# LSH attention, softplus-gated feed-forward and eight experts on one core: fewer weight blocks decoded during attention, feed-forward begun in two groups of two

## The chip, the cores and the metric

One core of a Trainium2 chip runs the whole program in one launch. The metric is device time in microseconds (us) of the launch; the kernel before takes 1490.02 us (median of 3 runs, 1488.71 to 1490.52). The engines are named as the profile names them: PE (matrix multiply, with PEld for its weight loads), DVE (vector), ACT (scalar, activations), POOL (GpSimd), SP (issues DMAs).

## The reference, cut to what matters

Three stages follow each other: hash-bucketed attention over 16 heads (2 x 8, 768 positions, 64 dimensions), a dense feed-forward whose two weight matrices arrive as float64, and eight experts weighted by a Sinkhorn-normalised gate.

```
mask   = q_bucket[..., :, None] == k_bucket[..., None, :]      # 6 sign bits
attn   = softmax(where(mask, q k^T / 8, -1e9))                 # + 1e-09 in the denominator
x      = (attn v) as [1536, 512]
h      = x @ w_in                                              # w_in  float64 [512, 2048]
x      = (h * tanh(softplus(h))) @ w_out                       # w_out float64 [2048, 512]
P      = sinkhorn(x @ w_gate, 8 rounds)
out    = sum over 8 experts of P[:, e] * (relu(x @ w1[e]) @ w2[e])
```

The change touches the attention and the feed-forward. The experts, which follow, are not touched.

## The kernel before, in words

**Attention.** Work is cut into 32 units (a head and one half of its 384 queries) and 16 pairs of units. Per unit, `s_mm` (L378, tile `ps`) and `s_max` (L383, `mx`) find the row maxima, `rows_mm`/`rows_cp` bring them into one row, `st_mm` (L413 and L414, `pst`) makes six blocks of transposed scores, `st_exp` (L419, ACT) writes their exponentials into a ring of NP tiles `p`, POOL adds three blocks at a time into `pa` (L431, `add`), and `av_mm` (L441, `pav`, twelve matmuls for a pair and half the keys) and `sum_mm` (L451, `psum`) multiply by v and by ones. `norm` then divides: part 0 transposes the sums, part 1 copies neighbouring 32-partition groups on ACT into `other` (L463), part 3 adds EPS, `other` and the own half and inverts (L465, L466), parts 4 to 7 spread, multiply and split the result into a rounded high part and the rest (`xh`, `xl`).

**What sets the order there.** The attention is a list of tasks with engine, cost, due time and predecessors; a planner inside the kernel simulates the engines and emits the tasks in the order of its simulated start plus DELTA times the due time. OFF holds an offset of the due time for each kind of task. So a change in OFF, DELTA, DUE0 or PACE moves instructions on every engine, and each engine then runs its queue in that order.

**Float64 blocks.** The feed-forward's weights are 16 blocks (128 hidden columns of `w_in`, the same rows of `w_out`). A block comes in two halves of 512 KB into `stage` (three buffers, next load issued when a half is decoded). `decode(i, j, part)` takes integers apart: parts 0 and 1 on ACT (L146, L148), parts 2 to 5 on DVE (L150, L152, L154, L158), part 6 on POOL (L160), part 7 a sum into `dec` (L162, DVE or POOL in attention, DVE later). When both halves are there, `convert_hi` (ACT, L174) rounds the block into the ring of weights, and `convert_lo` (POOL, L180) writes the rest beside it. The attention decodes NATT = 4 blocks, that is 8 halves, as tasks of its planner.

**Feed-forward.** Tokens are three tiles of 512 (`tb`), blocks are taken in groups of FG = 4. A step n is one block on one token tile: `up(n)` is 12 matmuls (L784 and L785 with the high part of the block, L786 with its low part) into `h`; `act(n)` runs Mish and the rounding on ACT (L794, L795, `gh`) and the difference on DVE (L796, `gl`); `down(n)` is 12 matmuls into four accumulators `y` (L809). `down` runs LAG = 3 steps behind `up`. After the last block of a group, `evacuate` moves the four `y` to `final`: by ACT copies for group 0 (L817), by DVE additions for later groups (L819). Here the order is that of the loops over n, word for word: decode parts of a half are put at the step `int(nd)`, where nd grows by 1.35 per half, and the conversion of a block at the end of a later step. In the loop:

```
        if n < NST:
            up(n)
            for t in early.pop(n, []):
                decode(*t)
        first = n >= LAG and step(n - LAG)[4]
        if first:
            down(n - LAG)
        if n < NST:
            act(n)
```

`first` is the case in which step n - 3 ends a group: its `down` and the evacuation then stand ahead of `act(n)`. Ahead of the loop, block 3 is converted.

Of the kernel before, what the change touches and what calls it, by code (L numbers as in the profile page):

```python
# [7 lines left out]
F32 = mybir.dt.float32  # L8
# [8 lines left out]
P = 128  # L17
# [19 lines left out]
NDEC = 4  # L37
NS = 4
NRAW = 2
NP = 13  # L40
NT3 = 3
NPA = 6
AVG = 3
AVD = 9
ENTER = 0.14
LEAVE = 0.2
TURN = 0.1
ADDS = "P"
ADDD = 2
WARM = 5  # L50
FILL = 256
AHEAD = (1, 2)
OFF = {'weight_lo': 36.6, 'add': -4.0, 'weight_load': -13.2, 'norm6': 47.2, 'prep_hi': 0.0, 'norm_move': -42.7, 'load_qk': 1.7, 'norm0': -50.6, 'load_v': -17.1, 'decode': 12.7, 'bits_mm': 4.7, 'norm1': -37.8, 'norm5': 6.7, 'st_exp': -4.0, 'norm7': 30.9, 'rows_cp': -121.7, 'av_mm': -0.2, 'rows_move': -14.2, 'rows_mm': 3.4, 'norm4': -154.4, 'norm3': 4.9, 'sum_mm': -2.0, 'bits_cmp': -19.3, 'av_one': -57.3, 'weight_hi': 177.8, 's_max': 3.7, 'st_mm': 2.6, 'prep_move': 0.2, 'prep_lo': 0.5, 'bits_move': -3.6, 's_mm': 3.0}
DELTA = 0.0397
RECEIPT = 1.6
DIRECT = 4
DUE0 = 20
PACE = 26
NX = 1
NATT = 4  # L60
# [13 lines left out]
def lsh_attention_moe_kernel(  # L74
# [111 lines left out]
    def attention():  # L186
        with ExitStack() as a:
# [23 lines left out]
            xu = out_p.tile([P, 2, HALF], F32, name="xu")  # L211
            rs = out_p.tile([P, S], F32, name="rs")
            nr = out_p.tile([P, HALF // 32], F32, name="nr")
            other = out_p.tile([P, HALF // 32], F32, name="other")
            pj = out_p.tile([P, 12], F32, name="pj")
            pf = sets.tile([P, 4, 32], F32, name="pf")

            ps = [p_p.tile([P, 512], F32, name=f"p{i}") for i in range(NP)]
            pas = [p_p.tile([P, HALF], F32, name=f"pa{i}") for i in range(NPA)]
            warm = []  # L220
            raw_t, hi_t, lo_t, psb_t, bit_t = {}, {}, {}, {}, {}
# [231 lines left out]
            def norm(n, part, e=None):  # L453
                hp, half = divmod(n, 2)
                b, hp = divmod(hp, H // 2)
                c, x = slice(half * HALF, (half + 1) * HALF), xu[:, half, :HALF]
                g = slice(b * S + half * HALF, b * S + (half + 1) * HALF)
                first = rs[:, c].rearrange("p (b j) -> p b j", j=32)[:, :, 0]
                if part == 0:
                    nc.vector.transpose(out=rs[:, c], in_=sum_t[n][:, :HALF])  # L460
                elif part == 1:
                    for y in range(4):
                        nc.scalar.copy(other[32 * y:32 * y + 32], first[32 * (y ^ 1):32 * (y ^ 1) + 32])  # L463
                elif part == 3:
                    nc.vector.scalar_tensor_tensor(out=nr, in0=other, scalar=EPS, in1=first, op0=ALU.add, op1=ALU.add)  # L465
                    nc.vector.reciprocal(out=nr, in_=nr)  # L466
                elif part == 4:
                    nc.vector.transpose(
                        out=rs[:, c].rearrange("p (b j) -> p b j", j=32),
                        in_=nr.unsqueeze(2).to_broadcast([P, HALF // 32, 32]),  # L470
                    )
# [96 lines left out]
            for u in range(NU):  # L568
# [14 lines left out]
                for c in range(NKC):  # L583
                    i = 6 * u + c
                    j = place(u, c) - NP
                    old = order[j + (NKC if j >= NKC else 0)] if u != 1 and j >= 0 else None
                    task("E", i - 4.0, st_mm, u, c, after=ready + ([nm(st_exp, *order[i - NT3])] if i >= NT3 else []) + [nm(bits_cmp, 0, 1, 0)] * (i == 2))
                    read = [av_done(old[0], old[1] // AVG), nm(add, old[0], old[1] // 3, max(old[1] % 3 - 1, 0))] if old else []
# [6 lines left out]
            for n in range(NU // 2):  # L595
                last = n == NU // 2 - 1
                us = members(n)
                due = 6 * us[1]
                room = [nm(norm, n - 1, 5)] if n else []
                for g in range(NKC // AVG):  # L600
                    task("E", due + AVG * g + AVD, av_mm, n, g,
                         after=[nm(st_exp, u, c) for u in us for c in range(AVG * g, AVG * g + AVG)] + ([nm(av_mm, n, g - 1)] if g else room)
                         + [nm(load_v, head(u)) for u in us] + [nm(clear_slots, j) for j in range(3)] * (n < 2))
                task("E", due + 8, sum_mm, n, after=[nm(add, u, g, 1) for u in us for g in range(2)] + [nm(norm, n - 2, 5)] * (n > 1), ring="r", frees=nm(norm, n, 0))
                raw = [nm(bits_mm, x) for x in (1, 2)] + [nm(prep_lo, x, i) for x in (1, 2) for i in range(2)]
                due += 10
                task("D", due, norm, n, 0, cost=0.58, after=[nm(sum_mm, n)] + ([nm(norm, n - 2, 5)] if n > 1 else raw))
                task("A", due, norm, n, 1, cost=0.85, after=[nm(norm, n, 0)] + [nm(norm, n - 1, 3)] * (n > 0))
# [17 lines left out]
            for n in range(NCH):  # L626
# [5 lines left out]
                for part, (e, cost) in enumerate(costs):  # L632
# [4 lines left out]
                        7: [nm(decode, i, j, 6)] + ([nm(weight_lo, i - NDEC, 1)] if i >= NDEC else []) + ([av_done(1, x) for x in range(NKC // AVG)] + [nm(add, 1, g, x) for g in range(2) for x in range(2)] if i < 3 else []),  # L637
                    }[part]
                    task(e, due + 0.3 * part, decode, i, j, part, after=after, cost=cost)
                if j == 1 and i < RING_A + NX:  # L640
                    last = uses(NH - NS + i - RING_A)[1]
                    task("A", due + 5, weight_hi, i, after=[nm(decode, i, x, 7) for x in range(2)] + ([nm(weight_lo, i - 1, 1)] if i else [])
                         + (st_done(last) if i >= RING_A else []))
# [48 lines left out]

            for k, t in tasks.items():
                for d in t[5]:
                    assert d in tasks, (k, d)
                    users.setdefault(d, []).append(k)
                if not left[k]:
                    ready_at[k] = 0.0
                    offer(k)
            count = 0  # L700
            while count < len(tasks):
# [13 lines left out]
                if e == "E":  # L715
                    mode[0] = KIND.get(f, 0)
                if e == "E" and nm(warm_up) in ends:
                    keep_warm(int(max(0.0, real - free[e] - 0.25) / 0.12))
# [14 lines left out]
                for d in users.get(k, ()):  # L733
                    left[d] -= 1
                    if not left[d]:
                        ready_at[d] = max(ends[x] for x in tasks[d][5])
                        offer(d)
                f(*args, *([e] if f in PICK else []))
                count += 1
# [24 lines left out]
    hps, hid, yps = {}, {}, {}  # L764
    NST = NTB * N64

    GROUPS = [list(range(i, i + FG)) for i in range(0, N64, FG)]
    NG = N64 // FG
    turns = [(g, tb) for g in range(NG - 2) for tb in range(NTB)]
    turns += [(g, tb) for g in (NG - 2, NG - 1) for tb in range(2)] + [(g, 2) for g in (NG - 2, NG - 1)]  # L770
    steps = [(g, tb, i) for g, tb in turns for i in GROUPS[g]]
# [253 lines left out]
    nxt = 0  # L1025
    nd = 0.0
    free_dec = {}
    convert_hi()
    convert_lo()
    for i in range(RING_A + NX + 1, N64):  # L1030
        need = free[i - RING] + 1 if i >= RING else 0
        if NATT <= i:
            nd = max(nd, free_dec.get(i - NDEC, 0))
            for j in range(2):
                d = int(nd)
                for part, lag in enumerate((0, 0, 0, 0, 0.5, 0.5, 0.5, 1.4)):
# [285 lines left out]
```

## Time and profile before

| what | value |
|---|---|
| median of 3 runs | 1490.02 us (1488.71 to 1490.52) |
| profiled execution | 1490.93 us, its span 1489.1 us |
| PE busy, share of the span | 1476.4 us, 99% |
| DVE, ACT, POOL busy | 871.2, 638.3, 913.9 us |
| attention (first instruction to the first `up`) | 0 to 222.97 us |
| granted PE clock, mean | 0.999 |

PE works nearly all the time, so the end moves by what PE waits, by the clock at which it runs, and by the number of its matmuls. The rows below show where it waits, and what DVE, POOL and ACT do ahead of the places that it may wait for. A matmul's duration covers its way through the array; what it takes of PE's time is the distance between starts.

### The profile page before, as it was taken

To read this page: it belongs to the slowest core of one execution; us is meant where nothing else is said; L and a number is where in the kernel's file an instruction comes from. 1 tells how busy PE (TensorE), PEld (TensorE's weight loads), DVE (VectorE), ACT (ScalarE), POOL (GpSimd) and SP (SyncE) were. 2 spreads that over 40 slices of the span, in tenths; PEclk is the share of its full clock that TensorE was granted. 3 is DMA by queue.
4 is the path that set the end of the run, shared out by engine and by line. 5 is a ranking of instruction groups with operands and counts; after the bars stand their busy time and mean duration, and the time that the engine had idled before them with its cause. 6 is when DMAs were issued, how large, how long until landed. Compare 5 with 4: busy or idle time off the path is not lost.

```text
span 1489.1 us, 20182 instructions
## 1 busy us (share of the span) xinstructions
PE 1476.4 (99%) x7457; PEld 1258.9 (85%) x7457; DVE 871.2 (59%) x1393; ACT 638.3 (43%) x1161; POOL 913.9 (61%) x762
## 2 busy tenths in 40 slices
PE   9999999999999999999999999999999999999998
PEld 6666658888888899998999989999899898998987
DVE  7898888777526666656444476643544435344353
ACT  6566656554324434344343333443334333343331
POOL 7878784333224766666666666666666666666660
PEclk9999999999999999999999999999999999999999
DMA  7755523222100122222122221232112221222211
GB/s 193 195 157 158 135 58 99 72 71 71 57 1 29 57 73 70 71 72 70 59 71 71 72 67 62 71 114 71 65 63 72 71 72 61 67 72 71 72 43 43
DMA packets 66490, 116.70 MB, mean 78 GB/s; under 512 B 18276, under 2 KB 20440, under 8 KB 66392
## 3 DMA queue, kind: packets, MB, share of 16 engines
q1 hardware_dynamic: 66392, 115.43, 25.4%
q8 instruction: 58, 0.95, 0.3%
q14 instruction: 40, 0.33, 0.1%
HBM read 93.41 MB, written 3.15 MB: 65 GB/s over the span
## 4 chain that ended last, share of the span: by engine, by line
PE 96%; DVE 2%; issue 1%; ACT 1%; DMA 1%; POOL 0%; DVEq 0%; ACTq 0%; SPq 0%; POOLq 0%
PE y L1174 35%; PE u L1107 32%; PE y L809 9%; PE pav L441 4%; PE h L786 3%; PE h L784 3%; PE h L785 3%; PE pst L413 2%; PE ps L378 2%; PE pst L414 2%; PE psum L451 1%; DVE mx L383 1%; PE pbits L352 0%; PE lg L837 0%; PE prow L394 0%
## 5 line engine op out<-in xcount | busy, mean ns | idle before, releaser
L1115 ACT ACTIVATE gh<-c 128x384 fp32r<-128x384 f32 x256 | 134.6, 526 | 174.3 <-DVE c L1127 172.2
L1127 DVE TENSOR_TENSOR u<-u,p 128x384 f32<-128x384 f32 x64 | 35.7, 558 | 283.7 <-PE u L1107 283.7
L1120 DVE SCALAR_TENSOR_TENSOR gl<-c,gh 128x384 fp32r<-128x384 f32 x256 | 196.0, 828 | 0.0
L1174 PE MATMUL y<-ww,gh 128*128 128x512 f32 x768 | 186.6, 391 | 0.0
L1174 PE MATMUL y<-w,gh 128*128 128x512 f32 x768 | 186.0, 391 | 0.0
L1174 PEld LDWEIGHTS y<-w,gh 128*128 128x128 f32 x768 | 143.7, 188 | 28.9
L1174 PEld LDWEIGHTS y<-ww,gh 128*128 128x128 f32 x768 | 143.7, 188 | 28.8
L989 POOL TENSOR_TENSOR w<-stage,w 128x1024 fp32r<-128x1024 f32 x32 | 76.3, 2385 | 89.1 <-ACT w L985 89.1
L989 POOL TENSOR_TENSOR ww<-stage,ww 128x1024 fp32r<-128x1024 f32 x32 | 76.3, 2384 | 81.7 <-ACT ww L985 81.7
L809 PE MATMUL y<-gh,w 128*128 128x512 f32 x336 | 109.8, 389 | 0.0
L160 POOL TENSOR_TENSOR stage<-stage,sgn 128x512 f32<-128x512 f32 x32 | 43.5, 1358 | 98.1 <-DVE sgn L158 74.4
L419 ACT ACTIVATE p<-pst 128x384 f32<-128x384 f32 x186 | 82.6, 490 | 46.8 <-PE pst L414 33.3
L985 ACT CAST ww<-stage 128x1024 fp32r<-128x1024 f32 x32 | 33.6, 1052 | 157.5 <-PE y L1174 157.5
L965 POOL TENSOR_TENSOR wa<-stage,wa 128x512 fp32r<-128x512 f32 x32 | 45.6, 1424 | 89.0 <-ACT wa L960 80.0
L985 ACT CAST w<-stage 128x1024 fp32r<-128x1024 f32 x32 | 33.6, 1050 | 154.5 <-PE y L1174 154.5
L1174 PE MATMUL y<-ww,gl 128*128 128x512 f32 x384 | 98.2, 389 | 0.0
L1174 PE MATMUL y<-w,gl 128*128 128x512 f32 x384 | 97.7, 389 | 0.2 <-DVE gl L1120 0.2
L965 POOL TENSOR_TENSOR wx<-stage,wx 128x512 fp32r<-128x512 f32 x32 | 45.4, 1419 | 80.6 <-ACT wx L960 80.6
L383 DVE TENSOR_REDUCE mx<-ps 128x1 f32<-128x768 f32 x96 | 88.3, 948 | 7.9 <-PE ps L378 6.8
L1107 PE MATMUL u<-tw,w 128*128 128x384 f32 x480 | 91.7, 336 | 0.0
L1107 PE MATMUL u<-tw,ws 128*128 128x384 f32 x480 | 91.7, 336 | 0.0
L1174 PEld LDWEIGHTS y<-w,gl 128*128 128x128 f32 x384 | 72.0, 188 | 15.5 <-DVE gl L1120 0.6
(206 smaller groups left out, 3651.1 us busy)
## 6 DMA issues: line engine op xcount, KB each, us to landing
stage<-in_w_dram SPq DMA_DIRECT2D x160, 512.0 KB
raw<-in_qk_dram SPq DMA_DIRECT2D x13, 384.0 KB
sb<-hi SPq DMA_DIRECT2D x20, 192.0 KB
vt<-in_v_dram SPq DMA_DIRECT2D x16, 192.0 KB
out_dram<-acc SPq DMA_DIRECT2D x11, 256.0 KB
wx<-hi SPq DMA_DIRECT2D x14, 192.0 KB
zq<-hi SPq DMA_DIRECT2D x10, 192.0 KB
ak<-hi SPq DMA_DIRECT2D x10, 192.0 KB
```

The costliest lines, as they stand in the source:

```text
L383: nc.vector.tensor_reduce(out=mx_t[u % 2][:, t:t + 1], in_=s_t.pop((u, t))[:, :, :HALF], axis=AX.XY, op=ALU.max, negate=True)
L419: nc.scalar.activation(p_t[u, c][:, :HALF], st_t.pop((u, c))[:, :HALF], AF.Exp, scale=0.125)
L441: nc.tensor.matmul(av_t[n][64 * e:64 * e + 64, :WIDE], vt[head(u) // 2 % 2][:, c, e, :], p_t[u, c][:, :WIDE], start=(c == 0), stop=(c == N ...
L784: nc.tensor.matmul(t, wt[:, 0, f], xh[:, kc, c], start=(kc == 0), stop=False)
L809: nc.tensor.matmul(yps[j], x, y, start=(head and m == 0), stop=(tail and m == 2))
L965: nc.gpsimd.tensor_sub(a[:, 1, 0:512], t[:, 0, :], f32(a)[:, 0, 0:512])
L985: nc.scalar.copy(wbuf[u % 2]["w"][:, 0, :], staged["u", u, 1].rearrange("p c n -> p (c n)"))
L989: nc.gpsimd.tensor_sub(y[:, 1, :], t, f32(y)[:, 0, :])
L1107: nc.tensor.matmul(bank[x], weight(u, a, m, kc), moving(u, b, mm, kc), start=(first and n == 0), stop=(n == 5), skip_group_check=not first)
L1115: nc.scalar.activation(hi, src, AF.Relu)
L1120: nc.vector.scalar_tensor_tensor(out=lo, in0=src, scalar=0.0, in1=f32(hid_u[u, c][0]), op0=ALU.max, op1=ALU.subtract)
L1174: nc.tensor.matmul(y_t[t], (hi, hi, lo)[m][:, t % 3 * P:(t % 3 + 1) * P], y, start=(k == 0 and first), stop=(k == NF // 2 - 1 and last),)
```

## The change

- The attention decodes and converts two blocks in place of four (NATT, and the task of block 2's conversion goes). Blocks 2 and 3 are decoded in the feed-forward loop; nd starts at block 2 and grows by 1.15 per half in place of 1.35. The conversion of block 3 ahead of the loop goes.
- The feed-forward's first group of four blocks becomes two groups of two: block 2 is first used in step 6, block 3 in step 7, block 4 in step 12 (as before) and block 7 in step 15 (as before). There are five groups and so three times four more evacuations; those of the second group are DVE additions, at steps 10, 12 and 14.
- `norm`: the ACT copies write beside the own half in `rs` and add EPS, and part 3 is one reduction over two neighbours; `other` is gone, and with it one wait of part 1.
- The ring of exponentials has 15 places, the two new ones in the fourth `dec` tile. The planner releases a place after the chunk of `av_mm` that reads it, and lets `av_mm` start up to a little ahead of its last exponentials. OFF, DELTA, DUE0 and PACE have new numbers; fewer filler matmuls are laid into PE's gaps in the first 7.5 us of the plan.

```diff
-NP = 13
+NP = 15
-OFF = {'weight_lo': 36.6, 'add': -4.0, 'weight_load': -13.2, ...
-DELTA = 0.0397
+OFF = {'weight_lo': 11.0, 'add': -10.2, 'weight_load': -52.8, ...
+DELTA = 0.0374
-DUE0 = 20
-PACE = 26
+DUE0 = 52
+PACE = 38
-NATT = 4
+NATT = 2
...
-            ps = [p_p.tile([P, 512], F32, name=f"p{i}") for i in range(NP)]
+            ps = [p_p.tile([P, 512], F32, name=f"p{i}") for i in range(NP - 2)] + [dec[3][:, k:k + 512] for k in (0, 512)]
...
-                        nc.scalar.copy(other[32 * y:32 * y + 32], first[32 * (y ^ 1):32 * (y ^ 1) + 32])
+                        z = 32 * (y ^ 1)
+                        nc.scalar.activation(both[32 * y:32 * y + 32, :, 1], both[z:z + 32, :, 0], AF.Copy, bias=EPS)
                 elif part == 3:
-                    nc.vector.scalar_tensor_tensor(out=nr, in0=other, scalar=EPS, in1=first, op0=ALU.add, op1=ALU.add)
+                    nc.vector.tensor_reduce(out=nr, in_=both, axis=AX.X, op=ALU.add)
...
+                    for c in range(AVG * g, AVG * g + AVG):
+                        for u in us:
+                            sooner[nm(av_mm, n, g), nm(st_exp, u, c)] = max(0.0, 0.66 * (c - AVG * g) - SLIP)
...
-                if j == 1 and i < RING_A + NX:
+                if j == 1 and i < RING_A:
...
-    GROUPS = [list(range(i, i + FG)) for i in range(0, N64, FG)]
-    NG = N64 // FG
+    GROUPS = [[0, 1], [2, 3]] + [list(range(i, i + FG)) for i in range(FG, N64, FG)]
+    NG = len(GROUPS)
...
-    convert_hi()
-    convert_lo()
-    for i in range(RING_A + NX + 1, N64):
+    for i in range(RING_A, N64):
...
-                nd += 1.35
+                nd += 1.15
```

Line numbers of the changed kernel are a little higher: L162 is its part 6 on POOL (before: L160), L182 its `convert_lo` (L180), L152, L154, L156, L160 its DVE parts 2 to 5, L164 its part 7, L810 its `gl`, L833 its evacuation by DVE.

**POOL at the start of the feed-forward, before.** `w_2662` and `w_2663` are the ring's places for blocks 4 and 5; the row ahead of these is the conversion of block 3.

```order
L160 TENSOR_TENSOR stage<-stage,sgn_86 128x512
L160 TENSOR_TENSOR stage<-stage,sgn_87 128x512
L160 TENSOR_TENSOR stage<-stage,sgn_86 128x512
L180 TENSOR_TENSOR w_2662<-dec_82,w_2662 128x1024
L160 TENSOR_TENSOR stage<-stage,sgn_87 128x512
L160 TENSOR_TENSOR stage<-stage,sgn_86 128x512
L160 TENSOR_TENSOR stage<-stage,sgn_87 128x512
L180 TENSOR_TENSOR w_2663<-dec_83,w_2663 128x1024
```

The same place in the changed kernel, behind the last `add` of the attention; `wx_78` takes block 2, `w_2614` block 3, `w_2615` block 4.

```order
L162 TENSOR_TENSOR stage<-stage,sgn_86 128x512
L162 TENSOR_TENSOR stage<-stage,sgn_87 128x512
L162 TENSOR_TENSOR stage<-stage,sgn_86 128x512
L162 TENSOR_TENSOR stage<-stage,sgn_87 128x512
L182 TENSOR_TENSOR wx_78<-dec_84,wx_78 128x1024
L162 TENSOR_TENSOR stage<-stage,sgn_86 128x512
L162 TENSOR_TENSOR stage<-stage,sgn_87 128x512
L182 TENSOR_TENSOR w_2614<-dec_85,w_2614 128x1024
L162 TENSOR_TENSOR stage<-stage,sgn_86 128x512
L182 TENSOR_TENSOR w_2615<-dec_82,w_2615 128x1024
```

Before, POOL reached block 4 first; now four halves (all of blocks 2 and 3) stand ahead of the conversion of block 2, and both halves of block 4 ahead of that of block 3.

**DVE in step 14 of the feed-forward, before** (from the `gl` of step 13 to that of step 14 and behind it); `dec_82` and `dec_83` are tiles of blocks 8 and 9, and no evacuation stands here.

```order
L796 TENSOR_TENSOR gl<-t,gh 128x512
L162 TENSOR_TENSOR dec_82<-stage 128x512
L154 SCALAR_TENSOR_TENSOR stage<-stage,sgn_86 128x512
L158 TENSOR_SCALAR sgn_86<-stage 128x512
L150 TENSOR_SCALAR stage<-stage 128x512
L152 TENSOR_SCALAR sgn_87<-stage 128x512
L796 TENSOR_TENSOR gl<-t,gh 128x512
L162 TENSOR_TENSOR dec_83<-stage 128x512
```

The same step in the changed kernel; `dec_85` belongs to block 7, `dec_82` to block 8, `sgn_87` in the last rows to the second half of block 8.

```order
L810 TENSOR_TENSOR gl<-t,gh 128x512
L164 TENSOR_TENSOR dec_85<-stage 128x512
L156 SCALAR_TENSOR_TENSOR stage<-stage,sgn_86 128x512
L160 TENSOR_SCALAR sgn_86<-stage 128x512
L152 TENSOR_SCALAR stage<-stage 128x512
L154 TENSOR_SCALAR sgn_87<-stage 128x512
L833 TENSOR_TENSOR acc<-y_3180,acc 128x512
L833 TENSOR_TENSOR acc<-y_3184,acc 128x512
L833 TENSOR_TENSOR acc<-y_3188,acc 128x512
L833 TENSOR_TENSOR acc<-y_3192,acc 128x512
L810 TENSOR_TENSOR gl<-t,gh 128x512
L164 TENSOR_TENSOR dec_82<-stage 128x512
```

Block 7's last sum has moved into this step's queue, two steps ahead of its first use, and four evacuations (the second group, third token tile) now stand among the decode parts. Behind the last row come parts 4 and 5 of block 8's second half.

**POOL around the conversions of blocks 6 and 7, before**; `w_2664` is block 6, `w_2665` block 7, and the L160 between them are the second half of block 7 and the first of block 8.

```order
L160 TENSOR_TENSOR stage<-stage,sgn_86 128x512
L180 TENSOR_TENSOR w_2664<-dec_84,w_2664 128x1024
L160 TENSOR_TENSOR stage<-stage,sgn_87 128x512
L160 TENSOR_TENSOR stage<-stage,sgn_86 128x512
L180 TENSOR_TENSOR w_2665<-dec_85,w_2665 128x1024
```

The same two conversions in the changed kernel; `w_2617` is block 6, `w_2618` block 7, and the L162 ahead of each are the two halves of blocks 7 and 8.

```order
L162 TENSOR_TENSOR stage<-stage,sgn_86 128x512
L162 TENSOR_TENSOR stage<-stage,sgn_87 128x512
L182 TENSOR_TENSOR w_2617<-dec_84,w_2617 128x1024
L162 TENSOR_TENSOR stage<-stage,sgn_86 128x512
L162 TENSOR_TENSOR stage<-stage,sgn_87 128x512
L182 TENSOR_TENSOR w_2618<-dec_85,w_2618 128x1024
```

Each conversion now stands behind a further half of the block that follows: that of block 7 behind the second half of block 8, whose DVE parts are put into step 14.

## Rows read from the trace of the kernel before

**Rows 1.** Windows: busy us and count of PE, PEld, DVE, ACT, POOL; PE clock; DMA.
```profile
0.00:222.97 222.97, 214.69 (x1290) 138.73 (x1290) 190.40 (x295) 135.74 (x311) 181.98 (x198) 0.99 0.58 150
222.97:260.00 37.03, 36.63 (x161) 29.97 (x161) 33.03 (x46) 24.25 (x42) 17.39 (x12) 1.00 0.30 95
62.00:66.00 4.00, 4.00 (x15) 3.69 (x14) 3.93 (x7) 2.58 (x5) 2.49 (x3) 0.57 0.70 248
```
**Rows 2.** Waits of PE in the attention: us in total, times, longest.
```profile
PE warm L292 <- DVE xh L286: 1.6, 1, 1.6
PE ps L378 <- DMA sb<-hi: 1.3, 1, 1.3
```
**Rows 3.** Timeline of PE in the attention: start us, duration us, instruction.
```profile
155.06 0.34 PE L413 MATMUL pst<-zq,ak 128*128 128x384 f32 x1
...
155.41 0.34 PE L413 MATMUL pst<-zq,ak 128*128 128x384 f32 x1
```
**Rows 4.** Groups of instructions in 0 to 223 us: count, busy us, mean ns.
```profile
L160 POOL TENSOR_TENSOR stage<-stage,sgn 128x512 f32<-128x512 f32 x7 | 9.9, 1413 | 1.6 <-DVE sgn L158 1.6
...
L154 DVE SCALAR_TENSOR_TENSOR stage<-stage,sgn 128x512 int32<-128x512 int32 x8 | 7.9, 984 | 0.1
...
L150 DVE TENSOR_SCALAR stage<-stage 128x512 f32<-128x512 f32 x8 | 6.4, 794 | 0.0
L152 DVE TENSOR_SCALAR sgn<-stage 128x512 int32<-128x512 int32 x8 | 6.3, 785 | 0.1
...
L158 DVE TENSOR_SCALAR sgn<-stage 128x512 int32<-128x512 int32 x8 | 6.1, 757 | 0.1
```
**Rows 5.** Chain of work in the feed-forward: start us, us, what.
```profile
234.82 2.72 PE y L809 x12
240.27 2.72 PE y L809 x12
```
**Rows 6.** Timeline of POOL in the feed-forward.
```profile
235.32 1.38 POOL L160 TENSOR_TENSOR stage<-stage,sgn 128x512 f32<-128x512 f32 x1 [3.15 <-ACT t L794]
239.48 1.31 POOL L160 TENSOR_TENSOR stage<-stage,sgn 128x512 f32<-128x512 f32 x1 [2.78 <-DVE sgn L158]
...
245.08 2.42 POOL L180 TENSOR_TENSOR w<-dec,w 128x1024 fp32r<-128x1024 f32 x1
...
260.42 2.40 POOL L180 TENSOR_TENSOR w<-dec,w 128x1024 fp32r<-128x1024 f32 x1
...
281.53 2.42 POOL L180 TENSOR_TENSOR w<-dec,w 128x1024 fp32r<-128x1024 f32 x1
```
**Rows 7.** Timeline of DVE in the feed-forward.
```profile
233.42 0.69 DVE L796 TENSOR_TENSOR gl<-t,gh 128x512 fp32r<-128x512 f32 x1 [0.51 <-ACT gh L795]
...
239.62 1.46 DVE L152 TENSOR_SCALAR sgn<-stage 128x512 int32<-128x512 int32 x1
...
317.14 2.73 DVE L819 TENSOR_TENSOR acc<-y,acc 128x512 f32<-128x512 f32 x4 [0.24 <-PE y L809]
319.79 0.68 DVE L796 TENSOR_TENSOR gl<-t,gh 128x512 fp32r<-128x512 f32 x1
320.39 0.69 DVE L162 TENSOR_TENSOR dec<-stage 128x512 f32<-128x512 f32 x1
320.99 0.69 DVE L154 SCALAR_TENSOR_TENSOR stage<-stage,sgn 128x512 int32<-128x512 int32 x1
321.71 0.43 DVE L158 TENSOR_SCALAR sgn<-stage 128x512 int32<-128x512 int32 x1
```
**Rows 8.** Timeline of ACT at the start of the feed-forward.
```profile
223.79 0.91 ACT L463 COPY other<-rs 32x12 f32<-32x12 f32 x4 [4.52 <-DVE rs L460]
...
230.84 1.28 ACT L794 ACT_TABLE_LOAD   x1
232.14 0.60 ACT L794 ACTIVATE t<-h 128x512 f32<-128x512 f32 x1
```

More of the change, by code (lines that the diff above doesn't have):

```diff
@@ L44 @@
 AVD = 9
+SLIP = 0.3
 ENTER = 0.14
@@ L50 @@
 WARM = 5
+COLD = 7.5
 FILL = 256
 AHEAD = (1, 2)
-OFF = {'weight_lo': 36.6, 'add': -4.0, 'weight_load': -13.2, 'norm6': 47.2, 'prep_hi': 0.0, 'norm_move': -42.7, 'load_qk': 1.7, 'norm0': -50.6, 'load_v': -17.1, 'decode': 12.7, 'bits_mm': 4.7, 'norm1': -37.8, 'norm5': 6.7, 'st_exp': -4.0, 'norm7': 30.9, 'rows_cp': -121.7, 'av_mm': -0.2, 'rows_move': -14.2, 'rows_mm': 3.4, 'norm4': -154.4, 'norm3': 4.9, 'sum_mm': -2.0, 'bits_cmp': -19.3, 'av_one': -57.3, 'weight_hi': 177.8, 's_max': 3.7, 'st_mm': 2.6, 'prep_move': 0.2, 'prep_lo': 0.5, 'bits_move': -3.6, 's_mm': 3.0}
-DELTA = 0.0397
+OFF = {'weight_lo': 11.0, 'add': -10.2, 'weight_load': -52.8, 'norm6': 87.2, 'prep_hi': 3.9, 'norm_move': -73.0, 'load_qk': -0.2, 'norm0': -29.7, 'load_v': -23.9, 'decode': -0.3, 'bits_mm': 4.8, 'norm1': -110.3, 'norm5': -85.1, 'st_exp': -3.3, 'norm7': 55.1, 'rows_cp': -157.2, 'av_mm': -0.1, 'rows_move': -39.6, 'rows_mm': 3.5, 'norm4': -106.6, 'norm3': 12.6, 'sum_mm': -2.3, 'bits_cmp': -16.6, 'av_one': 12.2, 'weight_hi': 293.4, 's_max': 6.6, 'st_mm': 2.5, 'prep_move': -6.4, 'prep_lo': -4.7, 'bits_move': -9.7, 's_mm': 2.4}
+DELTA = 0.0374
 RECEIPT = 1.6
 DIRECT = 4
-DUE0 = 20
-PACE = 26
+DUE0 = 52
+PACE = 38
 NX = 1
-NATT = 4
+NATT = 2
 FG = 4
@@ L213, in attention @@
             nr = out_p.tile([P, HALF // 32], F32, name="nr")
-            other = out_p.tile([P, HALF // 32], F32, name="other")
             pj = out_p.tile([P, 12], F32, name="pj")
             pf = sets.tile([P, 4, 32], F32, name="pf")
-            ps = [p_p.tile([P, 512], F32, name=f"p{i}") for i in range(NP)]
+            ps = [p_p.tile([P, 512], F32, name=f"p{i}") for i in range(NP - 2)] + [dec[3][:, k:k + 512] for k in (0, 512)]
             pas = [p_p.tile([P, HALF], F32, name=f"pa{i}") for i in range(NPA)]
@@ L457, in norm @@
                 g = slice(b * S + half * HALF, b * S + (half + 1) * HALF)
-                first = rs[:, c].rearrange("p (b j) -> p b j", j=32)[:, :, 0]
+                both = rs[:, c].rearrange("p (b j) -> p b j", j=32)[:, :, 0:2]
                 if part == 0:
@@ L514, in av_done, with av_chunk @@
                 return nm(av_mm, pair_of(u), g)
+            def av_chunk(n, c):
+                return "av_chunk", n, c
+            sooner = {}
             FAST = [("sq", 0)]
@@ L587, in attention @@
                     task("E", i - 4.0, st_mm, u, c, after=ready + ([nm(st_exp, *order[i - NT3])] if i >= NT3 else []) + [nm(bits_cmp, 0, 1, 0)] * (i == 2))
-                    read = [av_done(old[0], old[1] // AVG), nm(add, old[0], old[1] // 3, max(old[1] % 3 - 1, 0))] if old else []
+                    read = [av_chunk(pair_of(old[0]), old[1]), nm(add, old[0], old[1] // 3, max(old[1] % 3 - 1, 0))] if old else []
                     task("A", i - 9.0, st_exp, u, c, after=[nm(st_mm, u, c)] + read)
@@ L607, in attention @@
                 task("D", due, norm, n, 0, cost=0.58, after=[nm(sum_mm, n)] + ([nm(norm, n - 2, 5)] if n > 1 else raw))
-                task("A", due, norm, n, 1, cost=0.85, after=[nm(norm, n, 0)] + [nm(norm, n - 1, 3)] * (n > 0))
+                task("A", due, norm, n, 1, cost=0.85, after=[nm(norm, n, 0)])
                 task("D", due, norm, n, 3, cost=0.45, after=[nm(norm, n, 1)] + [nm(norm, n - 1, 4)] * (n > 0))
@@ L639, in attention @@
                     task(e, due + 0.3 * part, decode, i, j, part, after=after, cost=cost)
-                if j == 1 and i < RING_A + NX:
-                    last = uses(NH - NS + i - RING_A)[1]
-                    task("A", due + 5, weight_hi, i, after=[nm(decode, i, x, 7) for x in range(2)] + ([nm(weight_lo, i - 1, 1)] if i else [])
-                         + (st_done(last) if i >= RING_A else []))
+                if j == 1 and i < RING_A:
+                    task("A", due + 5, weight_hi, i, after=[nm(decode, i, x, 7) for x in range(2)] + ([nm(weight_lo, i - 1, 1)] if i else []))
                     for j in range(2):
@@ L694, in attention @@
                 for d in t[5]:
-                    assert d in tasks, (k, d)
+                    assert d in tasks or d[0] == "av_chunk", (k, d)
                     users.setdefault(d, []).append(k)
@@ L717, in attention @@
                 if e == "E" and nm(warm_up) in ends:
-                    keep_warm(int(max(0.0, real - free[e] - 0.25) / 0.12))
+                    keep_warm(int(max(0.0, real - free[e] - 0.25) / (0.21 if real < COLD else 0.12)))
                 if e == "Q":
@@ L732, in attention @@
                     ring_use[ring].append(frees)
-                for d in users.get(k, ()):
+                made = [k]
+                if f is av_mm:
+                    for x in range(AVG):
+                        made.append(av_chunk(args[0], AVG * args[1] + x))
+                        ends[made[-1]] = real + cost * (x + 1) / AVG + SEEN[e]
+                for d in (d for x in made for d in users.get(x, ())):
                     left[d] -= 1
                     if not left[d]:
-                        ready_at[d] = max(ends[x] for x in tasks[d][5])
+                        ready_at[d] = max(ends[x] - sooner.get((d, x), 0.0) for x in tasks[d][5])
                         offer(d)
@@ L778, in up @@
         g, tb, i, _, _ = step(n)
+        assert i < converted[0]
         wt = ring[i % RING]
```

## The prediction, made before the changed kernel ran

> **What bounds the kernel now.** I read the windows first. In the attention, 0 to 222.97 us, PE is busy for 214.69 us: it stands idle for 8.3 us in all [rows 1]. The waits of PE name them: the longest is 1.6 us for the first memset, which no edit touches; the next is 1.3 us for a DMA of `sb` [rows 2]. Between them PE is really fed: two neighbouring first matmuls of `pst` start 0.35 us apart, with the second one of the pair between them, shot after shot [rows 3]. So the attention holds at most 8.3 - 1.6 = 6.7 us of idle time to win. There is one stretch more: behind the DMA wait the granted clock falls, 0.57 on the mean of 62 to 66 us, so between the levels of 1.2 and 2.4 GHz, worth 4 x 0.43 = 1.7 us [rows 1].
>
> From 222.97 us on PE waits 0.4 us up to 260 [rows 1], and the chain shows `down` after `down` at a distance of 5.44 us: a step is 2.72 us of `up` and 2.72 us of `down`, 0.227 us per matmul [rows 5]. PE sets the end there, and every wait that is put into it is paid in full. I count time t from the first `up` (222.97).
>
> Third, the engines ahead of PE. DVE's parts 2 and 3 wait while POOL multiplies: L152 takes 1.46 us [rows 7] with the L160 of 1.31 us beside it [rows 6], where its sister L158 takes 0.43 [rows 7]. At the start of the feed-forward the two therefore work as one queue. One half of a block takes 4.16 us (L160 at 235.32, then 239.48); between the conversions of blocks 4 and 5, 245.08 and 260.42, three halves, one conversion and their `gl` take 15.34 us [rows 6].
>
> **Attention: what goes.** Four halves leave. DVE loses 4 x (0.984 + 0.794 + 0.785 + 0.757) = 13.3 us, POOL three of seven multiplications, 3 x 1.41 = 4.2 us: 17.5 us of the common queue [rows 4], and ACT loses parts 0 and 1. But PE hardly waited for that queue, so the gain is bounded by PE's own gaps: 6.7 + 1.7, and some 1.5 us of filler matmuls at the start (my estimate), about 10 us at best. The plan is reordered, which can open new gaps: 1 us of loss is the other end. I take 5 us, half of the bound, since the waits on `mx`, `row` and the exponentials are those of the order and not of the decode alone. The `norm` edit (a reduction over 128 x 24 for an addition over 128 x 12, on DVE), the two more places of `p` and the earlier release lie inside the same bound, off PE; I cost them at nothing, and what a longer reduction could cost, some 0.1 us in the last pair, is within the rounding.
>
> **Feed-forward: what comes.** First uses on PE: `up(0..2)` stand alone, then each step is 5.44, so step n begins at 8.16 + 5.44 (n - 3). Block 2 is needed at `up(6)`, t = 24.5, block 3 at 29.9, block 6 at 68.0, block 7 at 73.4, each plus 0.45 since the low part is first used by the third matmul. Before, block 7's low part was written from 281.53 to 283.95 [rows 6], t = 61: 12 us early. Now 17.5 us and the conversion of two blocks more lie ahead of it.
>
> *Block 2.* Before, DVE's first `gl` came at 233.42 [rows 7], and POOL began block 4's conversion 11.66 us later, behind three halves. Now ACT is done with `norm` at 224.70, does a half's parts (1.3), loads the table (1.28) and runs Mish and the rounding (2 x 0.6) [rows 8]: the first `gl` is at about t = 5.5. Four halves stand ahead of the conversion: 5.5 + 11.66 + 4.16 = 21.3, done at 23.7. It is needed at 24.95. No stall, by 1.2 us.
>
> *Block 3.* Two halves lie between, so 15.34 - 4.16 = 11.2 us later: 32.5, done at 34.9; put into DVE's queue instruction by instruction it comes a us earlier. Needed at 30.4: PE waits 3.5 to 4.5, I take 4.
>
> *Block 6.* Its conversion stands behind both halves of block 7, and those behind the evacuation at step 12, after `down(9)`. Counted from the end of `down(5)`: the ACT evacuation ends 0.8 us later (as DVE's does) and `act(8)` takes 1.2, so DVE resumes at +2.0. Up to the end of the conversion DVE and POOL then do 5 `gl` (3.0), 4 sums (2.4), parts 4 and 5 of 5 halves (5 x 1.12), parts 2 and 3 of 4 halves with POOL in the way (4 x 1.86), 2 evacuations (5.4), one last multiplication (1.4) and 2 conversions (4.8): 30.0 [rows 6, 7]. That is +32.0; PE comes there at 10 x 2.72 + 0.45 = 27.65. It waits 4.3 us. Were DVE on time, only the chain behind `down(9)` counts, as for block 7, and leaves 1.0.
>
> *Block 7.* Here the order alone decides. In step 14 DVE must do, behind `down(11)`: four evacuations, `gl`, a sum, parts 4 and 5 of block 8's second half; then POOL multiplies it and only then converts block 7. The same row of work before: evacuation from 317.14, L158 ends at 322.14 [rows 7], while that `down` ends at 234.82 + 15 x 5.44 + 2.72 = 319.1 [rows 5]; so +3.0, then 1.31 and 2.42 [rows 6] and 0.2 for hand-overs: 6.95 us behind `down(11)`. But `up(15)` follows it at once and wants the block after 0.45. PE waits 6.5 us, whatever the speed of DVE before; if DVE is late as for block 6, about a us more.
>
> Sum: 4 + 4.3 + 6.5 = 14.8 us. What such waits do to the clock: behind the wait of 1.3 us above, PE lost 1.7 us at the lower level [rows 1, 2]. I count that once for each of the three waits, 5.2 us; its bounds are 0 and 10. The 0.4 us of rows 1 goes. Feed-forward +19.6, attention -5: +14.6. The twelve additional evacuations cost PE nothing of themselves: the next `down` of a group's head comes 2.72 us later, and the first `y` is free 0.7 us after its evacuation begins.
>
> The skill speaks on the clock: the Trainium skill, "TensorE: Matmul & The Clock Gate", section "Why this matters for your kernels", advises against idle gaps between bursts of matmuls, since a long one puts the clock back to half. Rows 1 and 2 agree for a shorter gap than it names; by the rule all three waits pay, as in my sum, and without it the time would be about 1500.
>
> **Rivals.** *The common queue is the bound of the attention, not PE.* PEld is busy 138.73 of 222.97 us, while DVE is at 190.40 and POOL at 181.98 [rows 1]. If PE's busy time hides waits, all 17.5 us come back in the attention, and the feed-forward, with DVE on time, pays only what the order makes, 6.5 + 1.0: 1490.9 - 17.5 + 7.5 - 0.4 = 1480.5. It decides from where PE's matmuls start further apart than 0.35 us per pair. Against it: the rows of starts. The Trainium skill, "Trainium Kernel Development and Optimization", section "Performance Expectations", bears on this rival: matmul busy time is called a bad measure and the share of LDWEIGHTS a good one; by that, 0.62, PE has room and this rival's time would hold.
>
> *Decode keeps up.* If DVE and POOL interleave better than in rows 6, block 3 is in time and block 6 waits 1.0, the clock holds, and the attention gives 8: 1490.9 - 8 + 7.5 - 0.4 = 1490. For it: the reordering starts DVE 5 us earlier in the feed-forward. Against it: between 235 and 260 us DVE had no room.
>
> *The queue stays full.* From step 16 a block takes 2 x 3.5 + 2.4 of decode, 2.3 `gl` and 2.3/4 of an evacuation, 12.4 us, in 2.3 steps or 12.5 us (3.5 is 4.16 without its `gl`). If any of that is larger, later `gl` and evacuations come late too. Some 8 us more: 1512.5.
>
> **How the numbers follow.** 1490.93 + 14.6 = 1505.5 for the profiled execution, which lay 0.9 above the median of the runs: 1505. Chances: this 0.70 (1495 to 1514 by itself); the common queue 0.15; decode keeps up 0.08; the queue stays full 0.07. The range for 8 in 10 runs from 1489 (attention -10, feed-forward at 8) to 1515. A difference of 0.2%, 3 us, is what a measurement of this kernel tells from no change. Faster 0.16, the first rival and the edge of the second; the same 0.08; slower 0.76.
>
> **What would show it.** Right: the first `up` at 214 to 221 us; PE waiting in the third matmul of `up(7)`, `up(14)` and `up(15)` for POOL's conversion, the last of them 6 us or longer and there even if the other two are not; a granted clock under 1 behind them; no other wait up to the end. Wrong: a first `up` under 210 us (PE did wait for the queue), or blocks 6 and 7 converted ahead of the end of their `down`.

## The result, and the profile after

The changed kernel takes 1505.93 us (median of 4 runs, 1504.85 to 1507.45) against 1489.61 us (4 runs, 1488.71 to 1490.52): a ratio of 1.011, 95% interval 1.0093 to 1.0128. It is slower by 16.3 us; 1505 was forecast. The profiled execution took 1504.85 us, its span 1503.1 us, against 1490.93 and 1489.1 before: 14.0 us more of span, which the rows below account for.

First the waits of PE over the whole kernel (us in total, times, longest):

```profile
PE h L800 <- POOL w L182: 13.5, 3, 6.7
PE ps L379 <- DMA sb<-hi: 2.4, 1, 2.4
PE warm L293 <- DVE xh L287: 1.6, 1, 1.6
```

One row of three waits is new, and it holds 13.5 us: the third matmul of an `up` waits for POOL's `convert_lo`. The other two rows stood before as well [rows 2], the DMA's with 1.3 us. Nothing waits for the twelve additional evacuations.

The windows (busy us and count of PE, PEld, DVE, ACT, POOL; PE clock; DMA share; GB/s) of the attention, and of stretches behind the three waits:

```profile
0.00:219.66 219.66, 212.48 (x1285) 137.85 (x1285) 170.21 (x278) 129.77 (x302) 175.49 (x196) 0.99 0.57 147
256.00:258.00 2.00, 2.00 (x10) 1.66 (x9) 0.31 (x1) 1.57 (x3) 1.31 (x1) 1.00 0.67 250
296.00:298.00 2.00, 2.00 (x8) 1.56 (x7) 1.97 (x5) 0.00 (x0) 0.05 (x1) 0.64 0.19 23
298.00:300.00 2.00, 2.00 (x6) 1.55 (x5) 1.50 (x2) 0.59 (x1) 1.25 (x1) 0.51 0.66 240
310.00:312.00 2.00, 2.00 (x6) 1.52 (x6) 0.00 (x0) 0.00 (x0) 0.00 (x0) 0.50 0.00 0
312.00:314.00 2.00, 2.00 (x7) 1.57 (x6) 0.00 (x0) 0.00 (x0) 0.00 (x0) 0.59 0.00 0
```

Against [rows 1] the attention is 3.2 us shorter, counted to the first matmul of the first `up`, which stands at 222.90 before (the chain of work names 222.97) and at 219.66 now. DVE has 20 us less to do, POOL 6.5, yet PE's idle time only goes from 8.3 to 219.66 - 212.48 = 7.2 us. Behind the first wait the granted clock stays at 1.00; behind the second and the third it falls towards the half (1.2 of 2.4 GHz), 0.50 to 0.64, for about 4 us each: 2 x (0.36 + 0.49) + 2 x (0.50 + 0.41) = 3.5 us.

The three waits in PE's timeline (start us, duration us, instruction, wait ahead of it):

```profile
253.77 0.50 PE L800 MATMUL h<-xh,w 128*128 128x512 f32 x1 [3.44 <-POOL w L182]
...
295.56 0.50 PE L800 MATMUL h<-xh,w 128*128 128x512 f32 x1 [3.38 <-POOL w L182]
...
302.06 0.39 PE L823 MATMUL y<-gh,w 128*128 128x512 f32 x1
302.29 0.39 PE L798 MATMUL h<-xh,w 128*128 128x512 f32 x1
302.51 0.39 PE L799 MATMUL h<-xl,w 128*128 128x512 f32 x1
309.60 0.79 PE L800 MATMUL h<-xh,w 128*128 128x512 f32 x1 [6.70 <-POOL w L182]
```

These are `up(7)`, `up(14)` and `up(15)`, the first uses of blocks 3, 6 and 7. The chain that block 7 waited for: its last sum (DVE, step 14) and its rounding (ACT), then what DVE and POOL did ahead of its conversion:

```profile
295.98 0.68 DVE L164 TENSOR_TENSOR dec<-stage 128x512 f32<-128x512 f32 x1
...
300.44 2.74 DVE L833 TENSOR_TENSOR acc<-y,acc 128x512 f32<-128x512 f32 x4 [0.90 <-PE y L823]
303.09 0.68 DVE L810 TENSOR_TENSOR gl<-t,gh 128x512 fp32r<-128x512 f32 x1
303.69 0.69 DVE L164 TENSOR_TENSOR dec<-stage 128x512 f32<-128x512 f32 x1
304.30 0.69 DVE L156 SCALAR_TENSOR_TENSOR stage<-stage,sgn 128x512 int32<-128x512 int32 x1
305.01 0.43 DVE L160 TENSOR_SCALAR sgn<-stage 128x512 int32<-128x512 int32 x1
```
```profile
300.56 1.04 ACT L176 CAST w<-dec 128x1024 fp32r<-128x1024 f32 x1
```
```profile
305.96 1.29 POOL L162 TENSOR_TENSOR stage<-stage,sgn 128x512 f32<-128x512 f32 x1 [6.71 <-DVE sgn L160]
307.21 2.34 POOL L182 TENSOR_TENSOR w<-dec,w 128x1024 fp32r<-128x1024 f32 x1
```

Block 7's last sum is done at 296.66 and its rounding at 301.60. From then on POOL could convert it, but it stands idle for 4.36 us more (to 305.96), because the multiplication of block 8's second half stands ahead of the conversion in its queue; that waits for DVE's L160, which stands behind four evacuations. The conversion ends at 309.55; PE goes on at 309.60.

### The profile page after: what moved, and what is told of

It is laid out like the page before. It is cut to its first block, busy times and chain, and to the rows that moved or that the text cites. A ratio compares the mean times of both kernels' runs of the same rounds, so it can differ in the third digit from the quotient of the medians.

```text
span 1503.1 us, 20188 instructions
## 1 busy us (share of the span) xinstructions
PE 1478.4 (98%) x7452; PEld 1260.5 (84%) x7452; DVE 872.1 (58%) x1406; ACT 638.3 (42%) x1161; POOL 910.0 (61%) x762
## 4 chain that ended last, share of the span: by engine, by line
PE 94%; DVE 3%; DMA 1%; ACT 1%; issue 1%; POOL 1%; SPq 0%; DVEq 0%; POOLq 0%; ACTq 0%
PE y L1186 35%; PE u L1119 31%; PE y L823 7%; PE pav L442 4%; PE h L800 3%; PE h L798 2%; PE h L799 2%; PE pst L414 2%; PE ps L379 2%; PE pst L415 2%; PE psum L452 1%; PE pbits L353 1%; POOL w L182 0%; DMA sb<-hi 0%; DVE mx L384 0%
## 5 line engine op out<-in xcount | busy, mean ns | idle before, releaser
L162 POOL TENSOR_TENSOR stage<-stage,sgn 128x512 f32<-128x512 f32 x32 | 42.1, 1317 | 116.2 <-DVE sgn L160 91.6
L420 ACT ACTIVATE p<-pst 128x384 f32<-128x384 f32 x162 | 71.4, 490 | 51.3 <-PE pst L415 44.2
L810 DVE TENSOR_TENSOR gl<-t,gh 128x512 fp32r<-128x512 f32 x48 | 48.6, 1012 | 64.9 <-ACT gh L809 62.5
```

The source lines that it names most:

```text
L420: nc.scalar.activation(p_t[u, c][:, :HALF], st_t.pop((u, c))[:, :HALF], AF.Exp, scale=0.125)
L810: nc.vector.tensor_sub(lo, a, f32(hi))
```

## The experiments

Ratios are against the kernel before, run beside them: 1489.2 us (e1 to e4), 1489.82 (e5 to e8) and 1489.23 (e9 to e11).

**e1, conversions a step sooner** (all blocks, in the changed kernel):

```
-            need = max(need, d + 2)
+            need = max(need, d + 1)
```

> The changed kernel with each block converted one step sooner, at the end of the step in which its second half is summed, so that POOL's queue holds one multiplication of the following block less ahead of every conversion. Theory (the order of the queue makes the waits): the three waits of 3.4, 3.4 and 6.7 us in up(7), up(14) and up(15) go, and with them the two stretches of half clock (3.5 us); the first up stays at about 219.7 us; 1505.9 - 13.5 - 3.5 = 1489, or 1486 to 1490. Rival (the amount of work: six blocks cannot be decoded in time in any order): a wait of 3 us or more stays for block 6 or 7, 1495 to 1502.

1492.58 us, ratio 1.0022 (1.0013 to 1.0031). Between the two theories. The waits of PE:

```profile
PE h L800 <- POOL w L182: 3.2, 1, 3.2
...
PE y L823 <- DVE acc L833: 1.5, 1, 1.5
```

The waits for blocks 3 and 6 are gone, 3.2 us of block 7's stay, and one `down` now waits 1.5 us for its evacuation. So moving the conversions wins 13.4 us of the 16.7. What is left I put down to the amount of work that DVE and POOL have ahead of block 7; e6 below tests it.

**e2, block 7's conversion alone a step sooner:**

```
-            need = max(need, d + 2)
+            need = max(need, d + (1 if i == 7 else 2))
```

> The changed kernel with the conversion of block 7 alone one step sooner. Theory: the wait of 6.7 us in up(15) goes with its stretch of half clock (1.8 us), those of blocks 3 and 6 stay as they are: 1505.9 - 8.5 = 1497.4. Rival (the work that is late comes back at the next place): the wait moves to blocks 8 to 11 or to an evacuation, 1504 to 1506.

1496.96 us, ratio 1.0055 (1.0039 to 1.0071); the theory had 1497.4. The median is nearer to it than any run: the four lie at 1494.41, 1494.87, 1499.05 and 1500.33, at mean clocks of 0.998, 0.999, 0.994 and 0.993. The profiled one is 1494.41.

```profile
PE h L800 <- POOL w L182: 6.8, 2, 3.4
```

Block 7's 6.7 us is gone, the other two waits stand unchanged at 3.44 and 3.36. By the medians 9 us are won, of which the wait and the clock behind it would make 8.5.

**e3, the groups of two in the kernel before:**

```
-    GROUPS = [list(range(i, i + FG)) for i in range(0, N64, FG)]
-    NG = N64 // FG
+    GROUPS = [[0, 1], [2, 3]] + [list(range(i, i + FG)) for i in range(FG, N64, FG)]
+    NG = len(GROUPS)
```

> The kernel before with only the groups of the changed one, [0, 1] and [2, 3] in place of four blocks, all four still decoded in the attention. Theory: the twelve additional evacuations lie beside the matmuls, within 1 us of before, 1489 to 1491. Rival (evacuations hold up the next group's first matmuls): 12 x 0.7 = 8 us more, 1497.

1488.84 us, ratio 1.0003 (0.9993 to 1.0012). Twelve evacuations more cost nothing where blocks 2 and 3 are already decoded.

**e4, less decode in the attention of the kernel before:**

```
+        if i in (2, 3) and part in (2, 3, 4, 5, 6):
+            return
```

> The kernel before, its plan unchanged, with DVE's parts 2 to 5 and POOL's multiplication of blocks 2 and 3 left out (so their weights are not decoded). About 17.5 us of the common queue of DVE and POOL go from the attention. Theory (PE is the bound of the attention, it waits 6.7 us in all): the first up comes 1 to 4 us sooner, 1486 to 1489. Rival (the queue of DVE and POOL is the bound): the first up comes 10 to 17 us sooner, at 206 to 213 us, 1472 to 1480.

1488.84 us, ratio 0.9996 (0.9987 to 1.0005). Its attention in windows:

```profile
0.00:220.60 220.60, 213.37 (x1289) 136.47 (x1289) 175.18 (x279) 135.66 (x311) 177.26 (x197) 1.00 0.59 151
```

DVE is busy for 15 us less than in [rows 1], and PE's idle time is 220.60 - 213.37 = 7.2 us, just what the changed kernel has. The first `up` is 2.3 us earlier than in the profile before, but the time does not move: in e3, whose attention is that of before instruction for instruction, the first `up` came at 221.49, so 1.4 us of such a difference is one execution against another. This part of the decode is hidden behind PE.

**e7, the changed kernel with less DVE work ahead of block 8:**

```
+        if auto[0] and i < 8 and part in (2, 3, 4, 5):
+            return
```

> The changed kernel, order and conversions as they are, with DVE's parts 2 to 5 of blocks 2 to 7 left out in the feed-forward (so their weights are not decoded). Theory (the wait for block 7 is one of order, those for blocks 3 and 6 of the work ahead): the waits for blocks 3 and 6 go, that for block 7 stays at 4.5 to 6 us, since the evacuations, gl, a sum, the multiplication of block 8 and the conversion still follow down(11); 1495 to 1498. Rival (all three are the amount of work): no wait of over 1 us stays, 1488 to 1490.

1495.68 us, ratio 1.0038 (1.0023 to 1.0053), inside what the theory gave.

```profile
299.66 0.80 PE L802 MATMUL h<-xh,w 128*128 128x512 f32 x1 [6.01 <-POOL w L184]
```

The waits for blocks 3 and 6 go with DVE's work; block 7's stays at 6.0 us with most of that work gone. With DVE on time, the order alone makes it.

**e6, block 8 from step 16 on** (with e1's edit):

```
-            nd = max(nd, free_dec.get(i - NDEC, 0))
+            nd = max(nd, free_dec.get(i - NDEC, 0), 16 if i == 8 else 0)
```

> The first experiment (conversions one step sooner) with the decode of block 8 and behind held back to step 16, so that no part of block 8 stands ahead of block 7's conversion. Theory (what is left there is the amount of DVE and POOL work ahead of block 7, 3.2 us of wait, of which a multiplication of 1.3 us belongs to block 8): the wait in up(15) falls to 1 to 2 us, the wait of a down for its evacuation (1.5 us) stays, 1488 to 1491. Rival (the amount is not it, the wait is one of DMA or of ACT's order): the wait stays at 3 us, 1492.5.

1498.17 us, ratio 1.0061 (1.0046 to 1.0076), slower than e1 and outside both times that were expected.

```profile
296.95 0.50 PE L800 MATMUL h<-xh,w 128*128 128x512 f32 x1 [1.10 <-POOL w L182]
...
409.00 0.79 PE L798 MATMUL h<-xh,w 128*128 128x512 f32 x1 [3.06 <-ACT w L176]
```

Block 7's wait falls from 3.2 to 1.1 us, but the later blocks, all shifted, come late: `up` waits 3.1 us for ACT's conversion at 409 us. Work taken from ahead of one deadline stood ahead of the next.

**e5, three blocks in the attention** (with e1's edit):

```
-PACE = 38
+PACE = 26
-NATT = 2
+NATT = 3
```

> The changed kernel with three blocks decoded in the attention in place of two (its due times closer, PACE 26), and the conversions one step sooner as in the first experiment. Theory (decode is hidden in the attention, where PE is the bound, and not ahead of the feed-forward's blocks 3 to 7): the first up stays at 219 to 221 us, PE waits for no conversion, 1486 to 1488.5, below the kernel before. Rival (the attention pays for the decode): the first up moves to 224 us or later, 1490 to 1493.

1508.2 us, ratio 1.0124 (1.0109 to 1.0139): both theories missed. No `up` waits for a conversion any more (`down` waits 4.9 us in three places for ACT and for an evacuation), but the attention ends at 235.07 us, 15 us later than e1's (219.91). New in its waits:

```profile
PE pst L415 <- DMA sb<-row: 3.9, 1, 3.9
PE ps L379 <- DMA sb<-hi: 3.4, 1, 3.4
```

The edit holds two things, a third block's work and another PACE, which moves the due times and with them the loads of the weights. So:

**e11, PACE alone** (with e1's edit, two blocks):

```
-PACE = 38
+PACE = 26
```

> The first experiment (two blocks in the attention, conversions one step sooner) with PACE 26 in place of 38: the same work, only the due times of the weight loads and decode tasks closer, so that the loads stand elsewhere among SP's DMAs. It tells what cost the run with three blocks 15 us in the attention. Theory (the place of the loads in the plan, which the offsets were found for): the first up comes at 223 us or later with new DMA waits ahead of matmuls, 1496 or more. Rival (the third block's decode itself): the first up stays at 219 to 221, 1491 to 1494.

1501.04 us, ratio 1.0077 (1.0061 to 1.0093); the first `up` comes at 228.79. Of e5's 15 us some 9 come with PACE alone, at the decode work of two blocks, read from one profile of each. How the other 6 divide between the third block's work and the plan stays open.

**e8, the `norm` edit alone in the kernel before:**

```
-                        nc.scalar.copy(other[32 * y:32 * y + 32], first[32 * (y ^ 1):32 * (y ^ 1) + 32])
+                        z = 32 * (y ^ 1)
+                        nc.scalar.activation(both[32 * y:32 * y + 32, :, 1], both[z:z + 32, :, 0], AF.Copy, bias=EPS)
-                    nc.vector.scalar_tensor_tensor(out=nr, in0=other, scalar=EPS, in1=first, op0=ALU.add, op1=ALU.add)
+                    nc.vector.tensor_reduce(out=nr, in_=both, axis=AX.X, op=ALU.add)
```

> The kernel before with only the norm edit (EPS added by the ACT copies, the two partial sums in neighbouring columns, one reduction). Theory: off PE's path, within 1 us of before, 1488 to 1490.5; the reduction takes about the time of the addition that it replaces, or less. Rival (the reduction over columns that lie 32 apart is slower, 0.5 us or more, and holds up the last pair and the ring): 1492 or more.

1487.61 us, ratio 0.9983 (0.9974 to 0.9993): faster than both kernels, and the best version here, if by 2.5 us only. Its attention:

```profile
0.00:219.63 219.63, 212.51 (x1289) 136.38 (x1290) 188.14 (x295) 136.57 (x311) 182.29 (x198) 1.00 0.59 152
```

It ends as early as the changed kernel's (219.66), with all four blocks decoded in it.

**e9, the changed kernel with the old `norm`** (e8's edit undone):

> The changed kernel with the norm edit undone alone (a copy into a tile of its own, then one instruction that adds EPS and the two parts), plan and order as they are. Theory (the attention's 3 us came from the norm edit, since that edit alone made the kernel before 2 us faster and less decode made it no faster): the first up comes 2 to 4 us later than 219.7, at 221.5 to 224, the waits for conversions stay: 1508 to 1510. Rival (the gain came from the new plan, more places of p and less decode): the first up stays, 1505 to 1506.5.

1504.95 us, ratio 1.0101 (1.0086 to 1.0117). The time fits the rival: the runs lie at 1504.6, 1504.84, 1505.07 and 1507.57. The last is the profiled one, in which the first `up` comes at 221.60, 1.9 us later than in the changed kernel, as the theory had it. The same three waits of 13.5 us stand in both. In e9's trace PE waits 1.0 us more for DVE, for `mx` ahead of `ps` and for `xu` (2.1 us in place of 1.1), but its time is not longer than the changed kernel's: in the changed plan a gain of the `norm` edit is not shown.

**e10, e8 with fewer fillers** in PE's gaps of the first 7.5 us:

```
-                    keep_warm(int(max(0.0, real - free[e] - 0.25) / 0.12))
+                    keep_warm(int(max(0.0, real - free[e] - 0.25) / (0.21 if real < 7.5 else 0.12)))
```

> The kernel before with the norm edit and the smaller number of filler matmuls at the start, no other edit. Theory: as the norm edit alone, 1487.6, less what the fillers held up: 7 of 0.2 us less, of which at most 1 us reaches the first ps; 1486.5 to 1487.7. Rival (the fillers keep the clock up, without them the first matmuls run at half rate): 1488.5 to 1490.

1488.13 us, ratio 0.9989 (0.998 to 0.9998): no better than e8 (the intervals overlap). The 1.5 us that the prediction allowed for fillers do not show.

## Why the prediction was right

**The sum.** Its terms beside the spans of the two profiled executions:

| term | predicted, us | measured, us |
|---|---|---|
| attention | -5 | -3.2 |
| wait for block 3 | 4 | 3.44 |
| wait for block 6 | 4.3 | 3.38 |
| wait for block 7 | 6.5 | 6.70 |
| clock behind the waits | 5.2 | 3.5 |
| the 0.4 us of waits before | -0.4 | -0.4 |
| sum | 14.6 | 13.4; the spans differ by 14.0 |

The 0.6 us between 13.4 and 14.0 are not assigned. Attention and clock were off by 1.8 and 1.7 us with opposite signs, so the total was nearer than its terms.

**Feed-forward.** Place and cause were right. The first `gl` began at 225.32, t = 5.66 (predicted 5.5). The conversion of block 2 began at t = 21.1 (predicted 21.3), that of block 3 at 31.5 (32.5, "a us earlier"). POOL's timeline:

```profile
240.78 2.59 POOL L182 TENSOR_TENSOR wx<-dec,wx 128x1024 fp32r<-128x1024 f32 x1
...
251.19 2.53 POOL L182 TENSOR_TENSOR w<-dec,w 128x1024 fp32r<-128x1024 f32 x1
...
292.97 2.54 POOL L182 TENSOR_TENSOR w<-dec,w 128x1024 fp32r<-128x1024 f32 x1
```

So a half at the common rate of DVE and POOL, taken from the distance of conversions in [rows 6], carries over to halves in another place. Block 7 was worked out as 6.95 us behind `down(11)`. That ends about 302.3 and the conversion 309.55: 7.25, and the same chain step by step. e2 shows that its own place makes it, e7 that it stands without DVE's backlog too, e1 that the other two waits go with their place. So two causes work together for blocks 3 and 6, backlog (e7) and place (e1); either taken away removes the wait. For block 7 the place is enough; but in e1, where the other waits are gone and PE comes to it sooner, 3.2 us of wait are left with the place mended. Block 6 was mis-sized by 0.9 us: DVE was less behind than my +32.0 had it.

**Attention.** The size was off (3.2 us of 5), and what I had from less decode is not shown: e4 takes about the same work from DVE and wins nothing that can be measured. Nor does e9's time show that the changed kernel owes anything to the `norm` edit. The plan with its places of `p` and its earlier release is left, which no run tests by itself; what gives the 3.2 us stays open.

The step that failed is "off PE; I cost them at nothing", for the kernel before at least: there e8, the same `norm` edit, gives 2.5 us by itself (by its ratio; 1.0 to 3.9). The groups show what it replaced; before, then after, both over the attention (busy us, mean ns of one):

```profile
L465 DVE SCALAR_TENSOR_TENSOR nr<-other,rs 128x12 f32<-128x12 f32 x15 | 5.9, 392 | 1.6 <-ACT other L463 1.4
```
```profile
L467 DVE TENSOR_REDUCE nr<-rs 128x12 f32<-128x24 f32 x15 | 2.6, 171 | 2.7 <-ACT rs L465 2.5
```

I had expected the reduction to be 0.1 us longer; it is 0.22 us shorter in the mean. The last pair, for which I had allowed the 0.1 us, is not where it counts: the first `up` follows the last `psum` directly, and the last `norm` comes behind it (PE and DVE, before):

```profile
222.12 0.85 PE L451 MATMUL psum<-pa,ones 128*32 128x384 f32 x8
222.90 0.50 PE L784 MATMUL h<-xh,w 128*128 128x512 f32 x1
```
```profile
225.18 1.27 DVE L465 SCALAR_TENSOR_TENSOR nr<-other,rs 128x12 f32<-128x12 f32 x1
```

It counts where `norm` stands ahead of the row maxima in DVE's queue, and PE waits for those. The chain of work that ended last runs through the addition three times in the kernel before; the second time it goes on through the transpose and `mx` to PE (start us, us, what; then that wait in PE's timeline):

```profile
86.72 0.90 DVE nr L465
...
114.08 0.73 DVE nr L465
115.10 0.58 DVE rs L468
115.67 0.85 DVE mx L383
116.57 0.62 PE ps L378 x2
...
178.19 0.95 DVE nr L465
```
```profile
116.57 0.62 PE L378 MATMUL ps<-sb 96*128 96x384 f32 x2 [0.78 <-DVE mx L383]
```

In e3 the chain holds the addition four times, in e8 and e10 it holds no such row. Behind the three in the kernel before PE waits 0.44 us for `mx`, 0.78 for `mx` and 0.48 for `row`; of these e8 keeps 0.16 us (there the reduction takes 0.16 us) and e10 nothing. So 1.5 us of e8's gain stand in the rows. In its profile PE waits 0.7 us for ACT in a new place, so the sum for that execution is not closed.

An addition of twelve columns that takes 0.79 or 1.27 us mostly waits. The Trainium skill, "GPSIMD Engine Reference", section "1. Specifications", states that POOL shares its SBUF interfaces with VectorE, and names DVE instructions with two SBUF inputs, and those in a two-port mode, as the ones that contend. The trace agrees for the first kind: in the kernel before, the addition took 0.17 or 0.18 us in each of the seven places where POOL did nothing beside it, and 0.50 to 1.27 us in six of the seven where POOL worked beside it nearly throughout (0.19 in the seventh). The reduction, with one input, took 0.15 to 0.18 us in all 16 places, in 12 of them with POOL at work throughout. That a second input is not needed for a wait, L152 shows, which has one and takes 1.46 us beside POOL [rows 6, 7].

**Clock.** The direction was right and the size 1.7 us too large for the profiled execution: the first wait, 3.44 us, brought no fall, the second, 3.38 us, did. It differs from one execution to the next: in e2 the wait for block 3, again 3.44 us, was followed by a granted clock of 0.50 from 252 to 254 us and 0.79 up to 256, and in e9, where it was 3.41 us, by 0.50 from 256 to 258 and 0.77 up to 260, so in e9 all three waits paid. The changed kernel's own runs lie at 1504.85 and 1504.92 us (mean clock 0.995) and at 1506.95 and 1507.45 (0.993); whether the latter two paid for the first wait, no trace shows. The advice in the Trainium skill, "TensorE: Matmul & The Clock Gate", section "Why this matters for your kernels", to leave no gaps held for two waits of three in the profile of the changed kernel and for three of three in e9; by it alone all three would have paid.

**Rivals.** The common queue as the bound of the attention (1480.5) falls: e4 gives no gain from 15 us less of DVE, and the first `up` at 219.66 lies far from 205. Decode keeps up (1490) falls with the waits for blocks 3 and 6. The queue stays full (1512.5) falls: no row of waits names a later conversion or evacuation of the feed-forward, nor one of its `gl`. e6 shows, though, how near it was: with all later blocks shifted, one of them was 3.1 us late.

## What to carry to other kernels

Where an engine's queue is written out by hand, ask of each conversion or copy with a deadline what stands directly ahead of it in its own queue, and what that waits for: POOL idled 4.4 us with the data at hand because an instruction for a later block stood first, and moving the conversions by one step won 13.4 of 16.7 us. Work that leaves a stage bound by another engine wins nothing there that could be measured (e4), and costs where it lands ahead of a deadline. Test parts of a change alone: the one costed at nothing was the only one that made a kernel faster (e8); its instruction stood ahead of another that PE waited for.

## What the runs showed of the hardware that was not expected

- Waits of nearly equal length had different effects on the granted clock. Behind the wait for block 3 (3.41 to 3.44 us) it stayed at 1.00 in the changed kernel's profile and fell to 0.50 in those of e2 and e9. In the attention a DMA wait of 1.34 us was followed by 0.54 to 0.61 for 4 us before, one of 1.28 us in e2 by 1.00. The length of the wait alone does not tell; what else does stays open.
- One DVE addition of 128 x 12 with two SBUF inputs took 0.17 us with POOL idle and up to 1.27 us beside a working POOL; a reduction of 128 x 24 with one input took 0.15 to 0.18 us either way.
- One attention program shows first `up`s from 217.01 to 219.91 us in different executions (e2, e1, the changed kernel 219.66). Between e2 and the changed kernel a wait for one DMA makes 1.1 us of it (1.28 and 2.35), and the clock behind that wait 1.7 us (1.00 and 0.59, 0.56 from 88 to 92 us). A difference below 3 us there, read from one profile of each, says nothing of an edit.
- A move of the planner's due times with the same work (e11) made the attention 9 us longer: PE waited for an `issue` (2.6 us), for DVE's `xu` (2.6 in three waits) and for a DMA (1.2). In e5 such waits for DMAs reached 3.9 us, and the granted clock was 0.80 from 75 to 100 us and 0.86 from 150 to 175.
